# Keys and values of five of eight batches summed in pairs by accumulating DMAs instead of by GpSimd

## The chip, the cores and the metric

The kernel runs on one core of a Trainium2 chip. The metric is the device time of one execution in microseconds (us), told as the median of several runs; a profile is one further execution, and its span runs from the first to the last instruction. Engines are named as in the profile: PE is TensorE (matmuls; PEld its weight loads), DVE is VectorE, ACT is ScalarE, POOL is GpSimd, SP is SyncE. Each engine runs its own program strictly in order. DMAs issued by GpSimd or SyncE are carried out by 16 DMA engines that they share.

## What is computed

Inputs are q, k and v of shape 8 x 8 x 576 x 64 (batch, head, position, feature) in fp32, and four weight matrices. First comes attention with pooled keys and values, then a token and a channel MLP:

```python
k_p = k.reshape(B, H, Sp, pool, D).mean(axis=3)      # pool = 8, Sp = 72
v_p = v.reshape(B, H, Sp, pool, D).mean(axis=3)
scores = scale * np.matmul(q, k_p.transpose(0, 1, 3, 2))
...
attn = np.exp(scores)
attn = attn / (np.sum(attn, axis=-1, keepdims=True) + 1e-09)
attn_out = np.matmul(attn, v_p)
...
h = np.maximum(xt @ w_tok1, 0.0) @ w_tok2            # xt: x with tokens last
u = x + h.transpose(0, 2, 1)
h2 = np.maximum(u @ w_ch1, 0.0) @ w_ch2
out = u + h2
```

What matters here is the pooling: each pooled key (or value) is the mean of eight neighbouring rows of 64 numbers.

## The kernel before

**Units.** After a head for batch 0, the work goes in units 0 to 8. Unit n runs the channel MLP of batch n (`unit_steps`, matmuls of lines 438 and 461), 128x512 matmuls that fill TensorE. Unit 8 does the last tokens of all batches. Between its matmuls, a unit carries small steps of other batches: the attention and the token MLP of batch n+1, and the start of batch n+2. Tables (`FIRST` for unit 0, `SECOND` for unit 1, `THIRD` for unit 2, `LATER` from unit 3 on) say at which step of the unit which names are issued. A bare name means batch n+1, `<` batch n, `>` batch n+2; `lk3`, `lq3`, `lv3` mean the loads of k, q and v of batch n+3, `lv2` that of batch n+2. The order is written by hand (`manual_schedule`): every engine's program follows the order in which the steps are issued, and only the semaphores are put in by the framework.

**Loads.** `load_kv` fills a bf16 tile `kr` or `vr` of 72 partitions, with 8 heads x 8 rows x 64 numbers in each. Partition j holds the eight rows that pooled key j is made of. The load is one DMA, issued by GpSimd, that reads fp32 from HBM in pieces of 2,048 bytes and writes bf16 (line 86; batch 0 is cut in three). `load_q` loads q in the same way (line 103). Each of the three tiles has two buffers, so the load of batch b waits for the readers of batch b-2.

**Pooling.** `pool(eng, t, g)` pools four heads (g is 0 or 1) by `pool8`: add rows 0 to 3 to rows 4 to 7 (line 145, 72x1024 numbers out, fp32), add the halves of that (line 146, 72x512), and add the last two into `kp` or `vp` in bf16 (lines 149 and 151, 72x256). The names `K0 K1 V0 V1` do this on GpSimd, `k0 k1 v0 v1` on VectorE. VectorE does k1 and v1 of batch 1 and v1 of batch 2. From batch 3 on, all four are GpSimd's.

**Who needs it.** `kpT` (lines 194 and 196) transposes the pooled keys on TensorE and copies them to `kD` on VectorE; the scores `s0` to `s3` (line 254, exponent on ScalarE at line 260) read `kD` and the queries `qD` (line 243, `Q0` to `Q3`, VectorE). `av0` to `av4` (line 292) multiply the exponents by `vp`. All of these stand among the matmuls of the unit in TensorE's one program.

**GpSimd's program** around the change, from the tables: loads of batch 3 (FIRST step 20); K0, K1, V0 of batch 2 (FIRST steps 34 and 35); K0, K1 of batch 3 and the load of k of batch 4 (SECOND step 0); the loads of q and v of batch 4, then V0, V1 of batch 3 (SECOND step 1); then, in each of the units 2, 3 and 4, K0, K1, V0, V1 of batch n+2 and the loads of batch n+3 (step 0). GpSimd runs ahead of TensorE where nothing stops it. `spill` and `quads` (lines 372 and 379) move u through HBM in the later units, issued by SyncE: `mem` is written by one DMA and read by the next.

Of the kernel before, what the change touches and what calls it, by code (L numbers as in the profile page):

```python
# [8 lines left out]
FP32 = mybir.dt.float32  # L9
BF16 = mybir.dt.bfloat16  # L10
AF = mybir.ActivationFunctionType
ALU = mybir.AluOpType
# [8 lines left out]
def kernel(  # L21
# [14 lines left out]
    nc = tc.nc  # L36
    B, H, S, D = q.shape
    P = 128
    POOL = 8
# [40 lines left out]
    loaded = {}  # L80
# [4 lines left out]
    def kv(t, src, b, h0, h1, j0=0, j1=SP):  # L85
        nc.gpsimd.dma_start(out=t[j0:j1, h0:h1].rearrange("j h i d -> j h (i d)"),
                            in_=src[b, h0:h1].rearrange("h (j i) d -> j h (i d)", i=POOL)[j0:j1])

    def load_kv(b, src, key):
        t = loaded[b, key] = raw.tile([SP, H, POOL, D], BF16, name=key + "r")  # L90
        if b == 0:
            for h0, h1, j0, j1 in ((0, HP, 0, BP), (0, H, BP, SP), (HP, H, 0, BP)):
                kv(t, src, b, h0, h1, j0, j1)
        else:
            kv(t, src, b, 0, H)
# [12 lines left out]
    def load(key, b):  # L108
        if b < B:
            load_q(b) if key == "q" else load_kv(b, k if key == "k" else v, key)  # L110
# [31 lines left out]
    def pool8(eng, t, hs, dst, split):  # L142
        n = hs.stop - hs.start
        t4 = halves[eng is nc.vector]
        eng.tensor_tensor(out=t4[:, 0:n], in0=t[:, hs, 0:4], in1=t[:, hs, 4:8], op=ALU.add)  # L145
        eng.tensor_tensor(out=t4[:, 0:n, 0:2], in0=t4[:, 0:n, 0:2], in1=t4[:, 0:n, 2:4], op=ALU.add)  # L146
        if split:
            i0, i1 = (t4[:, 0:n, i].rearrange("j l (e d) -> j l e d", e=2) for i in range(2))
            eng.tensor_tensor(out=dst.rearrange("j e l d -> j l e d"), in0=i0, in1=i1, op=ALU.add)
        else:  # L150
            eng.tensor_tensor(out=dst, in0=t4[:, 0:n, 0], in1=t4[:, 0:n, 1], op=ALU.add)
# [3 lines left out]
    def batch_steps(b):  # L155

        par, first = b % 2, b == 0
        st = {}
# [26 lines left out]
        def pool(eng, t, g):  # L185
            def go():
                hs = slice(g * HP, (g + 1) * HP)
                pool8(eng, loaded[b, t], hs, st["kp"][:, g] if t == "k" else st["vp"][:, hs, 0:D], t == "k")
            return go

        def kpT():
# [383 lines left out]
```

## Time and profile before

| what | value | where from |
|---|---|---|
| median of three runs | 284.91 us (283.87 to 286.99) | the times |
| span of the profiled execution | 283.7 us | the page's first line |
| mean granted TensorE clock | 0.993 | the table of cores |
| DMA packets | 36,837, of which 18,672 on GpSimd's queue | the page's DMA part |
| HBM read, written | 38.21 MB, 11.80 MB | the page's DMA part |
| add of line 145 on GpSimd, keys, mean | 2,118 ns, 13 of them | the costliest groups |
| add of line 146 on GpSimd, mean | 1,332 ns, 25 of them | the costliest groups |
| add of line 149 on GpSimd, mean | 773 ns, 13 of them | groups by form |
| a load of k, q, v, issue to landing, median | 8.7, 11.9, 15.1 us | the DMA issues |

The page also shows the span in 40 slices of 7.1 us, each digit the busy share in tenths:

```profile
POOL 8684993999999929973993696000000000000000
PEclk9999979999999999999999999999999999999999
DMA  7999999951982397159748964514242346015014
```

GpSimd works in the first 25 slices and then has nothing left to do. The DMA engines are full for the first eight slices, while the weights and the first batches come in, and half full or less later. A line of the timeline begins with the start and the length in us; then come engine, line, operation, the tile that is written and those that are read, and in brackets how long the engine had been idle and what ended that. A line of the list of waits says who waited for what: us in total, times, longest.

### The profile page before, as it was taken

The page shows a single profiled execution, that of the slowest core. Times are in us where ns is not written, and L with a number is a line of the kernel's source. Part 1 is how long each engine was busy: PE and PEld are TensorE (multiplying, and loading weights), DVE is VectorE, ACT ScalarE, POOL GpSimd, SP SyncE. Part 2 cuts the span into 40 slices and gives each one's busy share as a digit, 9 for nine tenths or more (in the row PEclk, how much of TensorE's full clock was granted, in tenths as well). Part 3 has the DMA queues.
Part 4 walks back from the last instruction along what each step waited for, and adds up shares of the span by engine and source line. Part 5 has one row for each costly group of instructions (what it writes and reads, how often), then busy time and mean ns, then how long its engine had stood idle before and what let it go on. Part 6 is the DMA issues. An engine that isn't in the chain of part 4 may idle for free.

```text
span 283.7 us, 4529 instructions
## 1 busy us (share of the span) xinstructions
PE 273.8 (97%) x1816; PEld 130.9 (46%) x1816; DVE 149.4 (53%) x279; ACT 110.2 (39%) x193; POOL 138.1 (49%) x124
## 2 busy tenths in 40 slices
PE   8999879999999999999999999999999999999994
PEld 3855325443544445354435443544354444444443
DVE  5466975679657557474648464746474243011012
ACT  2543554009602643514561356135613511612600
POOL 8684993999999929973993696000000000000000
PEclk9999979999999999999999999999999999999999
DMA  7999999951982397159748964514242346015014
GB/s 158 193 202 208 204 202 186 217 121 40 124 138 64 74 127 126 37 78 200 162 75 137 231 165 52 112 39 122 45 96 55 102 64 136 16 37 112 2 39 109
DMA packets 36837, 32.68 MB, mean 115 GB/s; under 512 B 14288, under 2 KB 30288, under 8 KB 36816
## 3 DMA queue, kind: packets, MB, share of 16 engines
q0 software_dynamic: 18672, 17.64, 40.0%
q1 hardware_dynamic: 17984, 14.62, 21.8%
q8 instruction: 14, 0.23, 0.3%
q10 hardware_dynamic: 160, 0.13, 0.2%
q14 instruction: 7, 0.06, 0.1%
HBM read 38.21 MB, written 11.80 MB: 176 GB/s over the span
## 4 chain that ended last, share of the span: by engine, by line
PE 91%; DVE 5%; ACT 2%; issue 1%
PE p L461 31%; PE p L438 31%; PE p L353 6%; PE p L338 5%; PE p L254 4%; PE p L292 3%; PE pt L495 3%; ACT ex L260 2%; DVE qD L243 1%; PE pt L363 1%; DVE t L145 1%; PE p L450 1%; PE p L272 1%; PE p L321 1%; PE p L403 1%; PE p L225 1%
## 5 line engine op out<-in xcount | busy, mean ns | idle before, releaser
L461 PE MATMUL p<-w_ch,GT 128*128 128x512 bf16 x420 | 102.3, 380 | 0.0
L442 ACT ACTIVATE GT<-p 128x512 bf16<-128x512 f32 x108 | 64.3, 596 | 80.6 <-PE p L438 80.5
L438 PE MATMUL p<-uT,w_ch 128*128 128x512 bf16 x384 | 95.5, 382 | 0.0
L438 PEld LDWEIGHTS <-w_ch 128*128 128x128 bf16 x432 | 40.2, 98 | 47.9 <-issue 4.8
L461 PEld LDWEIGHTS <-GT 128*128 128x128 bf16 x420 | 37.6, 98 | 41.2 <-issue 3.5
L260 ACT ACTIVATE ex<-p 72x576 bf16<-72x576 f32 x56 | 33.1, 642 | 28.4 <-PE p L254 28.4
L145 POOL TENSOR_TENSOR t<-kr 72x1024 f32<-72x1024 bf16 x13 | 27.5, 2118 | 26.6 <-DMA kr<-in_k_dram 25.9
L466 DVE TENSOR_TENSOR o<-p,u 128x512 f32<-128x512 f32 x32 | 21.8, 682 | 32.3 <-PE p L461 32.2
L146 POOL TENSOR_TENSOR t<-t 72x512 f32<-72x512 f32 x25 | 33.3, 1332 | 2.0
L354 DVE TENSOR_TENSOR u<-p,x 128x512 bf16<-128x512 f32 x32 | 22.1, 691 | 13.7 <-PE p L353 13.7
L145 POOL TENSOR_TENSOR t<-vr 72x1024 f32<-72x1024 bf16 x12 | 25.5, 2123 | 0.8
L385 DVE STREAM_TRANSPOSE uT<-v 128x512 bf16<-128x512 bf16 x16 | 10.4, 685 | 22.0 <-DMA v<-mem 22.0
L310 DVE TENSOR_TENSOR x<-p,den 128x512 bf16<-128x512 f32 x30 | 20.7, 692 | 1.0
L243 DVE STREAM_TRANSPOSE qD<-qb 128x576 bf16<-128x576 bf16 x28 | 20.5, 789 | 0.0
L329 ACT ACTIVATE AT<-p 128x512 bf16<-128x512 f32 x8 | 4.8, 597 | 39.3 <-PE p L338 36.6
L292 PEld LDWEIGHTS <-ex 72*128 72x128 bf16 x320 | 15.4, 98 | 9.9 <-DVE x L310 0.8
L353 PE MATMUL p<-AT,w_tok 128*128 128x512 bf16 x64 | 19.0, 379 | 0.0
L292 PE MATMUL p<-vp,ex 72*128 72x65 bf16 x320 | 16.8, 194 | 0.5 <-DVE x L310 0.3
L254 PE MATMUL p<-qD,kD 32*72 32x288 bf16 x224 | 14.5, 306 | 2.0 <-DVE kD L196 1.8
L304 DVE RECIPROCAL den<-p 128x8 f32<-128x8 f32 (+1 forms) x39 | 8.0, 204 | 13.6 <-PE p L292 13.0
L338 PE MATMUL p<-x,w_tok 128*128 128x512 bf16 x56 | 14.4, 380 | 0.0
L331 DVE TENSOR_SCALAR AT<-p 128x512 bf16<-128x512 f32 x8 | 5.5, 692 | 13.7 <-PE p L338 12.9
(88 smaller groups left out, 207.3 us busy)
## 6 DMA issues: line engine op xcount, KB each, us to landing
out_dram<-o SPq DMA_DIRECT2D x70, 128.0 KB, 2.4
kr<-in_k_dram POOLq DMA_DIRECT2D x7, 576.0 KB, 8.7
qb<-in_q_dram POOLq DMA_DIRECT2D x7, 576.0 KB, 11.9
vr<-in_v_dram POOLq DMA_DIRECT2D x7, 576.0 KB, 15.1
w_ch<-in_moe_w_ch_dram POOLq DMA_DIRECT2D x6, 512.0 KB, 13.2
mem<-u SPq DMA_DIRECT2D x8, 256.0 KB, 2.1
v<-mem SPq DMA_DIRECT2D x8, 160.0 KB, 3.7
v<-mem SPq DMA_DIRECT2D x8, 128.0 KB, 3.4
```

The lines of the kernel that those rows point to most:

```text
L145: eng.tensor_tensor(out=t4[:, 0:n], in0=t[:, hs, 0:4], in1=t[:, hs, 4:8], op=ALU.add)
L146: eng.tensor_tensor(out=t4[:, 0:n, 0:2], in0=t4[:, 0:n, 0:2], in1=t4[:, 0:n, 2:4], op=ALU.add)
L243: nc.vector.transpose(out=late("qD")[:, g, db].rearrange("m (r j u) -> m u r j", u=2, r=BR), in_=st["qraw"][:, g].rearrange("m (u r d) -> ...
L254: nc.tensor.matmul(out=pss[l // 2][0:SP, l % 2, 0:SH], lhsT=st["kD"][quad, g, db, :], rhs=st["qD"][quad, g, db, half * SH:(half + 1) * SH] ...
L260: nc.scalar.activation(out=exv[:, h:h + 2], in_=pss[a][0:SP, :, 0:SH], func=AF.Exp, scale=scale)
L292: nc.tensor.matmul(out=halves[h // 4][:, (h % 4) * (D + 1):(h % 4 + 1) * (D + 1)], lhsT=st["ex"][:, h * S + n0:h * S + n0 + P], rhs=st["vp ...
L338: nc.tensor.matmul(out=ps, lhsT=w_tok1[:, c if c < 4 else 4 + par, m * P:(m + 1) * P], rhs=st["x"][:, c, :] if c < 4 else st["xt"], start= ...
L353: nc.tensor.matmul(out=ps, lhsT=w, rhs=a, start=(i == 0), stop=(i == len(mms) - 1))
L354: nc.vector.tensor_tensor(out=dst, in0=ps, in1=x, op=ALU.add)
L438: nc.tensor.matmul(out=ps, lhsT=w_ch1[:, kk, m * P:(m + 1) * P], rhs=uT[:, kk, :], start=(kk == 0), stop=(kk == 3))
L442: nc.scalar.activation(out=GT[:, m, :], in_=ps, func=AF.Relu)
L461: nc.tensor.matmul(out=ps, lhsT=GT[:, m, c * P:(c + 1) * P], rhs=w_ch2[:, m, :], start=(m == 0), stop=(m == NM - 1))
```

## The change

For batches 3 to 7, `load_kv` no longer loads bf16 rows. It sees the first half of the same tile as fp32, 8 heads x 128 numbers in a partition (`quarter_sums`). The eight rows of a pooled key are taken as four pairs; pair 0 is loaded by a plain fp32 DMA, and pairs 1, 2 and 3 are added to it by DMAs with `accum_op` add (`add_rows`). Each of these eight DMAs for k and v moves 72 x 8 pieces of 512 bytes. At the place of `lk3` only k's pair 0 is issued; at the place of `lv3` come v's pair 0 and then the six adds, k and v in turn. The load of q stays between them. In the tile then stand two sums of four rows, and `pool` does one add of 72x256 numbers, fp32 to bf16, on the engine that it had. Batches 0, 1 and 2 are as before.

```diff
+    summed = {}
+
+    def quarter_sums(b, key):
+        return loaded[b, key].rearrange("j h i d -> j (h i d)").bitcast(FP32)[:, 0:H * 2 * D].rearrange(
+            "j (h n) -> j h n", h=H)
+
+    def add_rows(b, key):
+        i = summed[b, key]
+        summed[b, key] = i + 1
+        src = (k if key == "k" else v)[b].rearrange("h (j i) d -> j h (i d)", i=POOL)
+        nc.gpsimd.dma_start(out=quarter_sums(b, key), in_=src[:, :, 2 * i * D:2 * (i + 1) * D],
+                            accum_op=ALU.add if i else ALU.bypass)
+
     def load_kv(b, src, key):
         t = loaded[b, key] = raw.tile([SP, H, POOL, D], BF16, name=key + "r")
+        if b >= 3:
+            summed[b, key] = 0
+            add_rows(b, key)
+            if key == "v":
+                for i in range(3):
+                    add_rows(b, "k")
+                    add_rows(b, "v")
+            return
...
         def pool(eng, t, g):
             def go():
                 hs = slice(g * HP, (g + 1) * HP)
-                pool8(eng, loaded[b, t], hs, st["kp"][:, g] if t == "k" else st["vp"][:, hs, 0:D], t == "k")
+                dst = st["kp"][:, g] if t == "k" else st["vp"][:, hs, 0:D]
+                if b < 3:
+                    pool8(eng, loaded[b, t], hs, dst, t == "k")
+                    return
+                pair = quarter_sums(b, t)[:, hs].rearrange("j l (i n) -> i j l n", i=2)
+                if t == "k":
+                    dst = dst.rearrange("j e l d -> j l e d")
+                    i0, i1 = (pair[i].rearrange("j l (e d) -> j l e d", e=2) for i in range(2))
+                else:
+                    i0, i1 = pair[0], pair[1]
+                eng.tensor_tensor(out=dst, in0=i0, in1=i1, op=ALU.add)
             return go
```

## The prediction

> **What bounds the kernel now.** I read the page's busy line first, then its chain of waits, then TensorE's waits after the start, and then GpSimd's timeline, because every line of the diff runs in GpSimd's program.
>
> ```profile
> PE 273.8 (97%) x1816; PEld 130.9 (46%) x1816; DVE 149.4 (53%) x279; ACT 110.2 (39%) x193; POOL 138.1 (49%) x124
> ...
> PE 91%; DVE 5%; ACT 2%; issue 1%
> ```
>
> TensorE is busy for 97% of the span and holds 91% of the chain; GpSimd (POOL) is busy for half. TensorE's waits from 45 us to the end, all that are over 150 ns:
>
> ```profile
> PE pt L194 <- DVE uT_tails L364: 0.5, 1, 0.5
> PE pt L194 <- DVE ex L166: 0.5, 1, 0.5
> PE pt L194 <- DVE uT L364: 0.2, 1, 0.2
> ```
>
> So after 45 us TensorE waits for 1.2 us in all. That caps what any relief of GpSimd or VectorE can bring at 1.2 us, or 0.4%. The waits before 45 us belong to batches 0 and 1, which the diff leaves alone. The question is only whether the change makes something late. GpSimd's timeline from 38 to 60 us:
>
> ```profile
> 38.58 1.59 POOL L151 TENSOR_TENSOR vp<-t 72x256 bf16<-72x256 f32 x1
> 40.12 0.86 POOL L86 DMA_DIRECT2D kr<-in_k_dram  x1
> 40.97 0.73 POOL L103 DMA_DIRECT2D qb<-in_q_dram  x1
> 41.68 0.84 POOL L86 DMA_DIRECT2D vr<-in_v_dram  x1
> 47.32 2.12 POOL L145 TENSOR_TENSOR t<-kr 72x1024 f32<-72x1024 bf16 x1 [4.79 <-DMA kr<-in_k_dram]
> 49.51 1.26 POOL L146 TENSOR_TENSOR t<-t 72x512 f32<-72x512 f32 x1
> 50.85 0.72 POOL L149 TENSOR_TENSOR kp<-t 72x256 bf16<-72x256 f32 x1
> 51.65 2.12 POOL L145 TENSOR_TENSOR t<-kr 72x1024 f32<-72x1024 bf16 x1
> ```
>
> The three issues are the loads of batch 3 (`lk3 lq3 lv3`, FIRST step 20). Behind them in the same program stand K0 and K1 of batch 2 (FIRST step 34). Each takes 4.1 us in three adds; K0 starts at 47.32, when its keys land, and K1 ends at 55.9. Who needs them, in the timeline around 63 us:
>
> ```profile
> 63.12 0.29 PE L194 MATMUL pt<-ident,kp 72*128 72x72 bf16 x4 [0.46 <-DVE ex L166]
> ...
> 63.45 0.31 DVE L196 COPY kD<-pt 128x288 bf16<-128x288 bf16 x1 [0.32 <-PE pt L194]
> ```
>
> This is kpT of batch 2, first in SECOND. TensorE runs its program in order, so all its work waits for K1 of batch 2. The slack there is 63.1 - 55.9 = 7.2 us. The same subtraction for the later batches, 3 to 7, with the ends of K1 at 70.1, 89.8, 114.7, 140.5 and 166.5 and their kpT at 88.2, 114.2, 139.6, 168.6 and 196.7, gives slacks of 18 to 30 us. Batch 2 is the tight place.
>
> **What is removed.** For batches 3 to 7, twenty pools lose their first two adds: 20 x (2.12 + 1.26) = 68 us of GpSimd work. It lies beside matmuls, and nobody on TensorE waits for it: worth 0 to 1.2 us by the waits above; I take 0. The one add left reads 72x256 fp32 pairs like line 149's row, 0.72 us, or 0.8 with the gap after it.
>
> **What is added.** Each batch has eight DMAs of 72 x 8 rows of 512 B in place of two, so GpSimd issues nine per batch with q's, five times. The issue of 576 rows costs 0.85 us now; six more are 5.1 us a batch. More important are the waits. An add must not start before the earlier transfer into the same bytes has landed. The trace shows an issuing queue doing just this where a DMA needs another's data (`v<-mem` after `mem<-u`):
>
> ```profile
> SPq L379 <- DMA mem<-u: 8.9, 4, 3.8
> ```
>
> I take it that GpSimd likewise stops, in its own program, until the earlier k or v part has landed, and everything behind it stops too. The Trainium skill's "DMA: Bandwidth & Descriptors", section "Rules for kernel authors", speaks against the change here: an accumulating DMA beside another access to the same bytes must wait for the earlier one's semaphore; no row of this trace shows an accumulating DMA.
>
> **Price of one add.** No such transfer is in the trace, so I bound it. Parts: k of batch 4, issued at 70.09 into idle queues, landed after 7.8 us, and batch 5's after 7.5. In the trace's packet records its 1024 B packets (2048 B read) take 98 ns each, and 15 engines work on them at once, 40 rows each: 3.9 us. The rest, about 3.7 us, is issue, start and receipt. Packets of 512 B that read 1024 B (line 121's) take 60 ns. On that straight line a plain row of 512 B takes 41 ns, so a first part is 40 x 41 = 1.6 us; an add reads 512 B and the old 512 B, so I take the 60 ns row: 2.4 us, and 3.7 + 2.4 = 6.1 us from issue to landing. Upper end: two reads one after the other, 120 ns, 4.8 us, landing 8.5 us. Lower end: the 256 KB of `mem<-u` land in 2.1 us, though from the SyncE queue and towards HBM. I take 6.1, since GpSimd-issued loads of the same rows are nearest.
>
> **Batch 3, step by step.** The queue is backed up at 40 us: v of batch 2, issued at 34.14, lands 17.0 us later, at 51.1 (the load's time to landing). Behind it: k's first part 52.7, q 56.0 (3.3 us, as batch 3's q lands after its k now), v's first part 57.6. Then, with each DMA issued when its predecessor has landed and the rings serving one after the other: k's first add 52.7 to 60.0, v's 57.6 to 63.7; k's second to 66.1, v's to 69.8; k's third issued at 66.1, v's at 69.8, done at 70.7. Only now does K0 of batch 2 start. K0 and K1 take what they take now, 55.9 - 47.3 = 8.6 us, and end at 79.3. kpT of batch 2 moves from 63.1 to 79.3: **16.2 us of TensorE idle**. Then comes the clock: after today's 2.9 us of TensorE waiting (34.6 to 37.4) the granted clock shows
>
> ```profile
> 37.00:40.50 3.50, 3.05 (x20) 0.83 (x20) 3.46 (x4) 1.67 (x3) 3.34 (x4) 0.51 1.25 205
> ```
>
> which is a stretch table whose third number from the end is the clock: half speed for 3.4 us. Matmuls after the new stall lose half of that, 1.7 us (0 if VectorE covers it). Sum 17.9 us.
>
> By the fit in the skill's same page, section "Anatomy of one DMA", 2.0 us plus bytes over 436 GB/s, an add of 295 KB would land in an estimated 2.7 us. The trace's 7.5 us for a load, of which 3.7 fixed, speaks for more; by the fit K0 would start near 64.9 and the sum would be 12 us, 297 in time.
>
> **What is late next.** V0 of batch 2 ends at 83.7, with av0 8.5 us behind kpT: hidden. K0 and K1 of batch 3, 1.6 us, end at 85.3. Then the load of batch 4 holds GpSimd: first parts at 90.6 and 95.5, v's adds 101.6 and 107.7, last issue done at 108.6. V0 and V1 of batch 3 stand behind it (SECOND step 1) and end at 110.1; their reader av0 is at 95.8 now, so at 113.7 then: hidden by 3.6 us only. From there a batch costs GpSimd 30.1 us (waits, issues, four adds) against about 28.5 us per batch on TensorE (kpT at 139.6, 168.6, 196.7). Batches 5, 6 and 7 are pooled at 141.8, 171.9 and 202.0 for kpT due at 157.5, 186.5 and 214.6: hidden by 16, 15 and 13 us. So TensorE pays once, in unit 1, and the shift stays to the end.
>
> **Sum.** Span 283.7 + 17.9 = 301.6. The runs' median, 284.91, lies 1.2 above the profiled span (which is near the lowest run, 283.87), so the time is **303 us**.
>
> **Rivals.**
> *GpSimd's chain binds later units too.* If one add needs over 7.9 us, the 3.6 us above are gone (two rounds stand in that sum, 1.8 us each). At 7.3 us a batch costs 33.7 and batch 7 alone is late, by 2 us: 308. At the upper end (4.8 us of transfer, so 9.6 us a round for k and v) a batch costs 40.6: the first stall is 23.2, av0 of batch 3 is 3.5 late, batches 6 and 7 about 11 each, with the clock's losses 55 in all: 340. For it: k and v share the rings, and SyncE's output stores, which the change leaves in place, take up to 0.3 of the same engines. Chance 0.2.
> *A short stall.* Adds land in 2.1 to 3 us, like `mem<-u`: K0 starts near 64, stall 9 to 11, 294 to 297. Against it stand the 7.5 us loads. Chance 0.08.
> *Not slower: the adds wait for nothing.* If the issues go out back to back, six more cost 5.1 us, GpSimd is free at 47.6 in place of 42.5, and K0 of batch 2, whose keys land at 47.2 anyway, starts 0.3 later, inside 7.2 us of slack. Time 284 to 285, at best 1.2 us lower. It decides if three rounds take less than about 13 us from 42.5 on, so that K0 starts before 54.5. The waits on `mem` speak against it; shorter work on GpSimd (49% busy, never the bound) speaks for it only if the waits fall away. Chance 0.08, of which 0.03 for over 1% faster, for which I see no row.
>
> **Numbers.** The forecast (one stall, 299 to 307) has 0.64. The range, 294 to 330, leaves out the rival with no waits and some of the short stall (about 0.1), and the upper part of the chain that binds (about 0.1). A measurement of this kernel tells about 1% from no change. Faster 0.03, same 0.05, slower 0.92.
>
> **What would show it.** In the changed profile: GpSimd idle between 42 and 70 us in waits for `kr` and `vr`; K0 of batch 2 starting near 70; kpT (line 194's successor) waiting for GpSimd by about 16 us, with a slice of low granted clock after it; no other TensorE wait over 2 us; GpSimd's work ending near 205. I am wrong if K0 of batch 2 still starts before 54, if an add lands outside 2 to 8.5 us, or if TensorE waits again at kpT of batches 6 and 7.

## The result, and the profile after

The changed kernel takes 312.06 us (median of four runs, 310.70 to 316.18); the kernel before, on the same chip, 285.95. The ratio is 1.090, with a 95% interval of 1.083 to 1.098: slower by 26 us. The medians here and below are over all runs of a kernel, while the ratios leave out, on both sides, runs that lie over 1.5% above their kernel's fastest. The profiled execution of the changed kernel spans 310.4 us, 26.7 more than before. All line numbers below are those of the changed kernel; line 225 is the old 194 (kpT), 323 the old 292 (av), 99 issues the new DMAs.

From the page, with cuts marked: busy time and count, the granted clock and the busy share of the DMA engines in 40 slices of 7.8 us, and the chain by engine.

```profile
PE 280.8 (90%) x1816; PEld 132.1 (43%) x1816; DVE 148.2 (48%) x279; ACT 110.4 (36%) x193; POOL 112.3 (36%) x114
...
PEclk9999869985599999999999999969999999999999
DMA  8999999994078989796999899991333263304114
...
PE 60%; DMA 16%; POOL 10%; issue 7%; DVE 4%; SPq 1%; ACT 1%; DVEq 0%; POOLq 0%
```

GpSimd has 26 us less to do, and TensorE, which held 91% of the chain, holds 60%: transfers and GpSimd stand in it now. The clock dips at slices 10 and 11 and again at slice 27; the dip at slices 5 and 6 lies in the head, where the kernel before has one at slice 6. TensorE's list of waits has grown at two places:

```profile
PE pt L225 <- POOL kp L170: 15.8, 3, 10.7
PE p L323 <- DVE x L341: 5.8, 3, 3.8
```

The first is kpT of batch 2 (14.7 of the 15.8; the rest is batch 1's, as before). The second is av in units 3 and 4: 1.6 and 3.8 us (the third wait, 0.3 us, is in the head). Subtracting the start of each batch's kpT before from that after (for batch 2 after, the start of its second half) shows where the time is lost:

| kpT of batch | before | after | later by | new in this stretch |
|---|---|---|---|---|
| 2 | 63.1 | 78.7 | 15.6 | the stall of unit 1 |
| 3 | 88.2 | 106.4 | 18.1 | 2.5, half clock after the stall |
| 4 | 114.2 | 132.3 | 18.1 | |
| 5 | 139.6 | 157.8 | 18.1 | |
| 6 | 168.6 | 188.6 | 20.0 | 1.8, wait at av in unit 3 |
| 7 | 196.7 | 223.5 | 26.8 | 6.8, wait at av in unit 4 and half clock |
| end of span | 283.7 | 310.4 | 26.7 | |

TensorE waits 14.7 us at kpT of batch 2; it had come to it 1.0 us later than before, out of the head.

**The first loss.** The timeline of GpSimd's program while it loads batch 3, up to the second half of kpT of batch 2:

```profile
41.90 0.85 POOL L99 DMA_DIRECT2D vr<-in_v_dram  x1
52.91 1.41 POOL L99 DMA_DIRECT2D kr<-in_k_dram  x1 [10.17 <-DMA kr<-in_k_dram]
55.85 1.39 POOL L99 DMA_DIRECT2D vr<-in_v_dram  x1 [1.53 <-DMA vr<-in_v_dram]
59.68 1.38 POOL L99 DMA_DIRECT2D kr<-in_k_dram  x1 [2.44 <-DMA kr<-in_k_dram]
62.47 1.39 POOL L99 DMA_DIRECT2D vr<-in_v_dram  x1 [1.41 <-DMA vr<-in_v_dram]
66.13 1.39 POOL L99 DMA_DIRECT2D kr<-in_k_dram  x1 [2.28 <-DMA kr<-in_k_dram]
68.72 1.37 POOL L99 DMA_DIRECT2D vr<-in_v_dram  x1 [1.20 <-DMA vr<-in_v_dram]
69.56 2.67 POOL L166 TENSOR_TENSOR t<-kr 72x1024 f32<-72x1024 bf16 x1
...
74.42 0.30 PE L225 MATMUL pt<-ident,kp 72*128 72x72 bf16 x2 [10.71 <-POOL kp L170]
...
78.74 0.30 PE L225 MATMUL pt<-ident,kp 72*128 72x72 bf16 x2 [4.02 <-POOL kp L170]
```

Each add waits for its own tile's transfer before (the brackets), and K0 of batch 2, the line at 69.56, stands behind all six. It started at 47.32 before.

**The second loss.** The chain of waits in unit 4, start and length:

```profile
185.62 5.08 DMA mem<-u
...
192.32 7.44 DMA v<-mem
...
199.88 0.16 DVE uT L416
...
204.28 0.70 DVE x L341
...
205.03 0.62 PE p L323 x8
```

u of batch 5 goes to HBM and back, which takes 14.1 us here, from the issue of the last `mem<-u` to the landing of the last `v<-mem`; it took 8.0 before (165.65 to 173.63). The DMA engines are fuller in this stretch: their busy share is 1.18 from 185.6 to 199.8 us (above 1 where packets overlap in time), and it was 0.67 before, from 165.6 to 173.7; for the round trip in unit 3 it is 1.02 where it was 0.64. VectorE waits for it in order (line 416). Its other work behind that, the division at line 341 among it, comes late, and av waits for the PSUM tiles that line 341 frees.

### The profile page after: what moved, and what is told of

It reads as the page before. It is cut to its first block, busy times and chain, and to the rows that moved or that the text cites. A ratio compares the mean times of both kernels' runs of the same rounds, so it can differ in the third digit from the quotient of the medians.

```text
span 310.4 us, 4512 instructions
## 1 busy us (share of the span) xinstructions
PE 280.8 (90%) x1816; PEld 132.1 (43%) x1816; DVE 148.2 (48%) x279; ACT 110.4 (36%) x193; POOL 112.3 (36%) x114
## 4 chain that ended last, share of the span: by engine, by line
PE 60%; DMA 16%; POOL 10%; issue 7%; DVE 4%; SPq 1%; ACT 1%; DVEq 0%; POOLq 0%
PE p L469 24%; PE p L492 21%; DMA v<-mem 5%; DMA vr<-in_v_dram 4%; DMA kr<-in_k_dram 4%; PE p L384 4%; PE p L369 4%; POOL t L166 3%; DMA mem<-u 2%; PE p L323 2%; PE p L285 2%; POOL t L167 2%; SPq L410 1%; DVE uT L416 1%; POOL vr L99 1%
## 5 line engine op out<-in xcount | busy, mean ns | idle before, releaser
L492 PE MATMUL p<-w_ch,GT 128*128 128x512 bf16 x420 | 104.6, 386 | 0.0
L469 PE MATMUL p<-uT,w_ch 128*128 128x512 bf16 x384 | 99.2, 393 | 0.0
L469 PEld LDWEIGHTS <-w_ch 128*128 128x128 bf16 x432 | 40.9, 100 | 50.3 <-issue 8.9
L99 POOL DMA_DIRECT2D kr<-in_k_dram x20 | 25.2, 1260 | 42.2 <-DMA kr<-in_k_dram 42.2
L99 POOL DMA_DIRECT2D vr<-in_v_dram x20 | 25.1, 1257 | 31.7 <-DMA vr<-in_v_dram 31.7
L323 PEld LDWEIGHTS <-ex 72*128 72x128 bf16 x320 | 15.8, 101 | 16.6 <-DVE x L341 7.9
L225 PE MATMUL pt<-ident,kp 72*128 72x72 bf16 x28 | 2.5, 203 | 16.5 <-POOL kp L170 15.8
L335 DVE RECIPROCAL den<-p 128x8 f32<-128x8 f32 (+1 forms) x39 | 7.9, 203 | 18.1 <-PE p L323 17.7
L362 DVE TENSOR_SCALAR AT<-p 128x512 bf16<-128x512 f32 x8 | 5.5, 691 | 13.4 <-PE p L369 12.6
```

Of the source, the lines that this page charges most:

```text
L99: nc.gpsimd.dma_start(out=quarter_sums(b, key), in_=src[:, :, 2 * i * D:2 * (i + 1) * D], accum_op=ALU.add if i else ALU.bypass)
L323: nc.tensor.matmul(out=halves[h // 4][:, (h % 4) * (D + 1):(h % 4 + 1) * (D + 1)], lhsT=st["ex"][:, h * S + n0:h * S + n0 + P], rhs=st["vp ...
L469: nc.tensor.matmul(out=ps, lhsT=w_ch1[:, kk, m * P:(m + 1) * P], rhs=uT[:, kk, :], start=(kk == 0), stop=(kk == 3))
L492: nc.tensor.matmul(out=ps, lhsT=GT[:, m, c * P:(c + 1) * P], rhs=w_ch2[:, m, :], start=(m == 0), stop=(m == NM - 1))
```

## The experiments

Each was run beside the kernel before on the same chip; the edits shown are against the changed kernel, with cuts marked. "Over before" is the difference of medians.

| run | median us | ratio to before, 95% interval |
|---|---|---|
| changed kernel | 312.06 | 1.090 (1.083 to 1.098) |
| from4 | 299.39 | 1.047 (1.039 to 1.055) |
| last_plain | 306.70 | 1.074 (1.067 to 1.082) |
| apart_plain | 295.79 | 1.034 (1.028 to 1.041) |
| busy | 313.97 | 1.100 (1.092 to 1.107) |
| two | 304.30 | 1.055 (1.046 to 1.065) |
| same_plain | 303.46 | 1.063 (1.055 to 1.071) |
| order | 300.28 | 1.052 (1.045 to 1.060) |
| first_parts67 | 308.02 | 1.083 (1.075 to 1.091) |
| no_spill34 | 306.97 | 1.075 (1.065 to 1.085) |
| from4_v | 299.99 | 1.040 (1.028 to 1.052) |
| busy2 | 314.50 | 1.097 (1.087 to 1.107) |
| both_out | 288.70 | 1.011 (1.004 to 1.018) |

**from4: batch 3 as before.**

```diff
-        if b >= 3:
+        if b >= 4:
...
-                if b < 3:
+                if b < 4:
```

> Adds for batches 4 to 7 only; batch 3 is loaded and pooled as before. Theory A (TensorE's stall in unit 1 comes from batch 3's waiting adds, which stand ahead of K0 and K1 of batch 2 in GpSimd's program): K0 of batch 2 starts near 47 again, the 14.3 us stall and its 3 us of half clock go, and what stays is the later loss of about 8 us: 8 to 10 over before, 294 to 296. Rival B (the adds' transfers slow the whole kernel through the DMA engines, wherever they stand): four fifths of the 26 us stay, near 307. Rival C (the later loss follows from the first stall): 286 to 288.

Measured: 299.39, 12.7 over before. K0 of batch 2 starts near 46 and the stall at its kpT is gone, so theory A holds for this stall, and B and C fall. But the time is 3 us above A's upper end. TensorE's waits in this run:

```profile
PE p L323 <- POOL vp L172: 5.6, 2, 4.0
PE p L323 <- DVE x L341: 4.8, 3, 3.8
```

The first line is new: av of batch 3 now waits for V0 and V1 of batch 3, which stand behind the load of batch 4 (SECOND step 1) and still take three adds each. That is the same mechanism, one batch on, with half clock for 6.8 us (95.8 to 102.7).

**last_plain: batches 6 and 7 as before.**

```diff
-        if b >= 3:
+        if 3 <= b < 6:
...
-                if b < 3:
+                if not 3 <= b < 6:
```

> Adds for batches 3 to 5 only; 6 and 7 are loaded and pooled as before. Theory D (the two waits of TensorE at av in units 3 and 4, 1.6 and 3.8 us, and the half clock after the second, 3 us, come from the round trip of u through HBM, v<-mem, which is carried by the same DMA engines while the adds of batches 6 and 7 run): those waits go, v<-mem lands within 9 us of the last mem<-u again, the stall of unit 1 stays: 17 to 19 over before, 303 to 305. Rival (they come from GpSimd's late pools or from the first stall): 311 to 313.

Measured: 306.70, 20.0 over before, 1.7 us above the range. kpT of batch 2 comes 16.3 us later than before, much as in the changed kernel. The waits at av shrink to 1.0 and 1.3 us, with no half clock after them, but they don't go, and the round trips take 11.9 and 11.6 us, not 9: plain loads of 1.2 MB of fp32 each also stood in the rings (the queues of the DMA engines) while u went out (`mem<-u` issued at 152.7 landed at 160.1).

**apart_plain: no part waits for another.**

```diff
...
-        nc.gpsimd.dma_start(out=quarter_sums(b, key), in_=src[:, :, 2 * i * D:2 * (i + 1) * D],
-                            accum_op=ALU.add if i else ALU.bypass)
+        dst = quarter_sums(b, key, i) if i < 2 else apart[key, i].rearrange("j (h n) -> j h n", h=H)
+        nc.gpsimd.dma_start(out=dst, in_=src[:, :, 2 * i * D:2 * (i + 1) * D],
+                            accum_op=ALU.bypass)
```

> Batches 3 to 7: all four parts of k and v are plain DMAs into four places of their own, so that no part waits for another; the bytes read and the number of DMAs stay. The sums over the four parts are left out: the one add pools the first part alone. Theory A (the waits between the adds are the cost): GpSimd is held only by the issues and the eight-deep queue, K0 of batch 2 starts at 51 to 55 and its K1 ends by 63: no stall in unit 1, 286 to 291. Rival B (number of DMAs and bytes): 305 to 312.

Measured: 295.79, 9.1 over before. The step in question came out as theory A said: the last issue of batch 3 starts at 53.3 and TensorE waits 1.4 us at kpT of batch 2 in place of 14.7. The total missed A's range by 4.8 us, and one wait of 6.8 us at av in unit 3, with half clock after it, is more than that: the eight plain DMAs now stand in the rings together, and one `v<-mem`, issued at 141.5, landed at 155.6. So the second loss needs no accumulating DMA.

**busy and busy2: TensorE kept busy through the stall.**

```diff
-    SECOND = {0: "kpT Q0 Q1 >K0 >K1 lk3", 1: "Q2 Q3 v1 lq3 lv3 >V0 >V1", 4: "s0", 6: "s1", 9: "s2", 12: "s3", 14: "av0", 16: "av1",
+    SECOND = {0: "w60 kpT Q0 Q1 >K0 >K1 lk3", 1: "Q2 Q3 v1 lq3 lv3 >V0 >V1", 4: "s0", 6: "s1", 9: "s2", 12: "s3", 14: "av0", 16: "av1",
...
+                if s[0] == "w":
+                    head("d" + s[1:])
+                    continue
```

> As changed, with 60 matmuls of 128x512 without use (12.9 us at full clock) ahead of kpT at the start of unit 1, inside the stall of 14.3 us. If the half clock after the stall costs 3 us (6 us of matmuls at half rate after 78.7), the clock stays full and the time falls by 2.5 to 3.5 us against the changed kernel, to 308 to 310. If VectorE covers that stretch, as my lower bound had it, the time stays at 311 to 313.

Measured: 313.97, no gain, and inconclusive: the added matmuls ended before the second part of the stall, and the clock fell in it and stayed at half from 77.5 to 84.3. busy2 therefore also puts 21 matmuls between the two halves of kpT of batch 2.

```diff
...
             for i in range(4):
+                if b == 2 and i == 2:
+                    idle = ps_one.tile([P, 512], FP32, name="p1")
+                    for _ in range(21):
+                        nc.tensor.matmul(out=idle, lhsT=warm[:, 0:P], rhs=warm, start=True, stop=True)
```

> The changed kernel with matmuls without use both ahead of kpT of batch 2 (60) and between its first and second pair of transposes (21, 4.5 us), so that TensorE is busy through both parts of the stall. The clock should stay full after 78 (it fell in the run with the first 60 alone, in the second part of the stall). If the half clock costs about 3 us: 308.5 to 310.5; if VectorE covers that stretch: 311.5 to 313.

Measured: 314.50, outside both ranges, so the total decides nothing. The stretch does. In busy2 the window from 78 to 107 us shows (clock third from the end):

```profile
78.00:107.00 29.00, 28.76 (x204) 13.68 (x203) 17.38 (x31) 11.69 (x21) 18.49 (x15) 1.00 0.51 83
```

From the last transpose of kpT of batch 2 to that of batch 3 it takes 25.1 us (81.9 to 107.0), exactly as before the change (63.2 to 88.3), against 27.7 in the changed kernel (78.8 to 106.5). The half clock costs 2.6 us, and VectorE does not cover it. In this execution the stall itself ended 3 us later, and the waits at av took 2.7 and 4.1 us in place of 1.6 and 3.8: what was gained in one place was lost in others.

**two: one round of adds.**

```diff
...
-        nc.gpsimd.dma_start(out=quarter_sums(b, key), in_=src[:, :, 2 * i * D:2 * (i + 1) * D],
+        nc.gpsimd.dma_start(out=quarter_sums(b, key), in_=src[:, :, 4 * i * D:4 * (i + 1) * D],
...
-                for i in range(3):
+                for i in range(1):
...
-                pair = quarter_sums(b, t)[:, hs].rearrange("j l (i n) -> i j l n", i=2)
+                t4 = halves[eng is nc.vector]
+                four = quarter_sums(b, t)[:, hs].rearrange("j l (i n) -> j l i n", i=4)
+                eng.tensor_tensor(out=t4[:, :, 0:2], in0=four[:, :, 0:2], in1=four[:, :, 2:4], op=ALU.add)
+                pair = [t4[:, :, i] for i in range(2)]
```

> Batches 3 to 7 in two parts of four rows (pieces of 1,024 B): one plain load and one add for k and for v, and two adds of GpSimd left in place of one. Theory A (the number of rounds that GpSimd waits through sets the stall): the first parts land by 57, one add each, K0 of batch 2 starts near 59, its K1 ends near 67.5: kpT of batch 2 about 4.5 later than before in place of 15.6; with up to 3 us of half clock and 1 to 4 us at the spills 6 to 11 over before, 292 to 297. Rival (an accumulating transfer is slow in itself, by its bytes): the same bytes are added, the stall shrinks by less than half, 302 or more.

Measured: 304.30, with runs from 298.89 to 307.72 (the profiled one is the fastest); a miss. kpT of batch 2 is 8.6 later than before, not 4.5. The first part of v (576 KB) landed at 61.4, where that of 288 KB had landed at 55.6, and the adds of 576 KB took 10.7 and 8.1 us to land. So rounds are not all: part of an add's price grows with its bytes (the first of the two also ran beside the end of v's first part). Yet with one round in place of three kpT of batch 2 came 7.0 us earlier than in the changed kernel (15.6 to 8.6 late). TensorE's wait there shrank by less, from 14.7 to 10.2, because in this execution it came to it 2.5 us earlier.

**same_plain: the waits without the adding.**

```diff
-                            accum_op=ALU.add if i else ALU.bypass)
+                            accum_op=ALU.bypass)
```

> All eight DMAs of a batch plain, each part into the same place as the one before it, so the waits stay and nothing is added; the sums over the parts are left out (the last part alone is pooled). If the wait for a landing is most of the price and the adding itself little: each part lands in about 4.5 us like k's first part in place of 6.0 to 6.4, and its issue takes 0.85 in place of 1.39: K0 of batch 2 starts near 66, kpT of batch 2 is 11 to 12 later than before, in all 15 to 20 over before, 301 to 306. If the adding is most of it: parts land in under 3 us, the stall is below 6, under 296.

Measured: 303.46, within the range. Issues take 0.81 us, k's parts land in 4.9 to 5.3 us, and kpT of batch 2 is 12.3 later than before. Of 15.6 us, the adding, with its longer issues and landings, accounts for 3.3, the waits for landings for most of the rest (apart_plain, without them, leaves 1.4 us of waiting).

**order: the pools first.**

```diff
-             16: "s0", 18: "s1", 20: "s2 lk3 lq3 lv3", 22: "s3", 24: "av0", 26: "av1", 28: "av2", 30: "av3", 32: "av4",
-             34: "at0 >K0 >K1", 35: "at1 >V0", 37: "u0", 38: "u1", 39: "u2", 40: "t0", 41: "u3", 42: "t1 u4", 44: "t2", 45: "t3",
+             16: "s0", 18: "s1", 20: "s2", 22: "s3", 24: "av0", 26: "av1", 28: "av2", 30: "av3", 32: "av4",
+             34: "at0 >K0 >K1", 35: "at1 >V0 lk3 lq3 lv3", 37: "u0", 38: "u1", 39: "u2", 40: "t0", 41: "u3", 42: "t1 u4", 44: "t2", 45: "t3",
...
-    SECOND = {0: "kpT Q0 Q1 >K0 >K1 lk3", 1: "Q2 Q3 v1 lq3 lv3 >V0 >V1", 4: "s0", 6: "s1", 9: "s2", 12: "s3", 14: "av0", 16: "av1",
+    SECOND = {0: "kpT Q0 Q1 >K0 >K1 lk3", 1: "Q2 Q3 v1 >V0 >V1 lq3 lv3", 4: "s0", 6: "s1", 9: "s2", 12: "s3", 14: "av0", 16: "av1",
```

> The change, with the loads of batch 3 moved behind K0, K1 and V0 of batch 2 (FIRST step 35), and V0, V1 of batch 3 ahead of the loads of q and v of batch 4 (SECOND step 1). Theory A: K0 of batch 2 starts near 47, no wait at its kpT. But batch 3's load then begins at 60, and GpSimd's chain (29 to 34 us a batch) has lost the slack that the first stall gave it: TensorE waits a few us each at kpT of batches 4 to 7, in all 9 to 16 over before, 295 to 302. Rival (order does not matter, the work of the adds does): 311 to 313. If GpSimd's chain stays hidden as the prediction had it (slack of 13 us or more): the spills alone, 291 to 295.

Measured: 300.28, 15.0 over before, within A's range. K0 of batch 2 is on time, and the waits move on:

```profile
PE pt L225 <- POOL kp L219: 9.2, 4, 4.3
PE p L323 <- DVE x L341: 2.1, 2, 1.6
```

The first line is kpT of batches 5 and 7, up to 4.3 us each: GpSimd takes 31 to 33 us from the load of one batch to the next (83.9, 115.5, 146.7, 179.3), TensorE 28 to 29 before the change. Batch 4's load starts at 83.9, close to the changed kernel's 85.8, while TensorE is some 18 us earlier here (kpT of batch 3 at 87.8, not 106.4). The prediction's hidden 13 to 16 us were there only because the first stall held TensorE back.

**first_parts67: little traffic for batches 6 and 7.**

```diff
-            if key == "v":
+            if key == "v" and b < 6:
```

> The change, but for batches 6 and 7 only the first part of k and v is loaded, the adds are left out (so their pooled values are of two rows). Theory D (traffic of batches 6 and 7 delays the round trip of u): with a quarter of that traffic v<-mem lands within 9 us of the last mem<-u, as before, no wait at av in units 3 and 4, the stall of unit 1 stays: 17.5 to 20 over before, 304 to 306; below the run with plain loads for batches 6 and 7 (306.7), which still waited 1.0 and 1.3 us there. Rival (those waits have another cause on VectorE): both waits stay, 309 to 312.

Measured: 308.02, between the two ranges. The wait in unit 4 is gone (`v<-mem` 193.3 to 198.8 with no load beside it), but the one in unit 3 grew to 4.2 us: without batch 6's adds, GpSimd issued batch 7's load at 158.6, right beside `v<-mem` (158.4 to 170.2). The trace's packet records show the two side by side: from 162 to 166 us, 498 packets of 256 B of `v<-mem` next to 220 of 2,304 B and 38 of 4,096 B, 125 small packets a us; before the change, alone in the rings, some 430 a us (2,560 from 168 to 174). I had reduced the traffic, and moved the rest to the worst moment. The load beside it here is plain, as in apart_plain and last_plain: the round trip is slowed by loads without adds too.

**no_spill34: u not through HBM in units 3 and 4.**

```diff
+    MIDDLE = {i: " ".join(x for x in s.split() if x[0] not in "MT") for i, s in LATER.items()}
+    for i, x in ((6, "t0"), (7, "t1"), (9, "t2"), (13, "t3"), (16, "t4")):
+        MIDDLE[i] = (MIDDLE.get(i, "") + " " + x).strip()
...
-            unit(n, LATER)
+            unit(n, MIDDLE if n in (3, 4) else LATER)
```

> The change, but u of batches 4 and 5 is transposed by TensorE in units 3 and 4 (steps t0 to t4, as units 1 and 2 do) and no longer goes through HBM there. Theory D (the waits at av in those units come from v<-mem, held up in the DMA rings by whatever load runs beside it): no wait at av in units 3 and 4, no half clock after 200; kpT of batch 2 as late as in the changed kernel (15 to 16). The transposes cost TensorE about 0.22 us for each of 9 blocks, 2 us in all. 18 + 2 = 20 over before, 304 to 307, 5 to 7 below the changed kernel. Rival (the waits come from GpSimd or from VectorE's own work): the waits stay, 312 to 315.

Measured: 306.97, at the top of the range. The stall of unit 1 stays (kpT of batch 2 is 17.5 us later than before, batch 3's load having been issued 1.9 us later than in the changed kernel), the waits at av in units 3 and 4 are gone (the 0.3 is in the head), and the clock is full from 85 us to the tail:

```profile
PE pt L225 <- POOL kp L170: 17.6, 3, 11.9
...
PE p L323 <- DVE x L341: 0.3, 1, 0.3
```

The batches' adds and GpSimd's waits are as in the changed kernel; the round trip is taken away, for TensorE's transposes. From kpT of batch 2 to the end, 4.3 us are lost against the kernel before in place of 11.1: 2.0 in the half clock after the stall and 2.3 between kpT of batches 4 and 6, where the transposes stand. This settles theory D.

**from4_v: V0 and V1 of batch 3 ahead of the load of batch 4.**

```diff
-        if b >= 3:
+        if b >= 4:
...
-                if b < 3:
+                if b < 4:
...
-    SECOND = {0: "kpT Q0 Q1 >K0 >K1 lk3", 1: "Q2 Q3 v1 lq3 lv3 >V0 >V1", 4: "s0", 6: "s1", 9: "s2", 12: "s3", 14: "av0", 16: "av1",
+    SECOND = {0: "kpT Q0 Q1 >K0 >K1 lk3", 1: "Q2 Q3 v1 >V0 >V1 lq3 lv3", 4: "s0", 6: "s1", 9: "s2", 12: "s3", 14: "av0", 16: "av1",
```

> Adds for batches 4 to 7 only, as in the run before (299.4), and V0, V1 of batch 3 moved ahead of the loads of q and v of batch 4 (SECOND step 1). Theory A, extended: the waits of 1.5 and 4.0 us at av of batch 3 and the half clock there (3 us) came from these pools standing behind the adds of batch 4; they go, the later waits (0.7 and 3.8 us and 1.7 of clock) stay: 5 to 8 over before, 291 to 294. Rival (they have another cause): 298 to 301.

Measured: 299.99, a miss, in the rival's range, though the rival's reason does not hold: the waits at av of batch 3 did go. Those of units 3 and 4 grew to 4.4 and 8.2 us in the profiled execution (301.19, the slowest of the four; the fastest took 295.93), with half clock after both: loads and round trips now coincide (one `v<-mem` took 14.7 us to land, the longest seen). The price of the second loss depends on when they meet.

**both_out: both causes removed, adds kept for batches 4 to 7.** Its edits are those of from4_v and no_spill34 together.

> The last two together: adds for batches 4 to 7 only, V0 and V1 of batch 3 ahead of the loads of batch 4, and u of batches 4 and 5 transposed by TensorE in units 3 and 4. If the two causes (pools of an earlier batch behind waiting adds in GpSimd's program; v<-mem held up by loads in the DMA rings) are all of the loss, TensorE waits nowhere over 1 us after 60 us and the clock stays full: 2 us of transposes and nothing else, 1 to 4 over before, 287 to 290, though 36 DMAs of adds and their waits are still made. If something else in the adds costs time, 293 or more. It does not beat the kernel before by either theory.

Measured: 288.70, 3.9 over before; within the range. From TensorE's list of waits:

```profile
PE p L285 <- DVE kD L227: 2.0, 1, 2.0
PE pt L225 <- POOL kp L170: 1.3, 1, 1.3
...
PE p L323 <- DVE x L341: 0.6, 1, 0.6
```

All three lie in the head, before 40 us (at 38.5, 35.3 and, 0.55 of the last, 18.6); after 60 us no wait is over 0.6 us, and the clock stays full from 44 us to the tail. The accumulating DMAs of four batches (24; the 36 of the expectation counts all that GpSimd issues for them), and GpSimd's waits for them, are still there and cost nothing that shows: of the 4.2 us by which the profiled span is longer than before, 1.9 arise in the head, before kpT of batch 2, 2.3 between kpT of batches 4 and 6, where the transposes stand, and none anywhere else. No version here beats the kernel before.

## Why the prediction was right or wrong

**Direction and first loss: right, by its own steps.** GpSimd stops for each landing; K0 of batch 2 starts at 69.6 (predicted 70.7); kpT of batch 2 is 15.6 us late (16.2). from4, order and apart_plain each took away one condition of this step (batch 3's adds, their place, their waits), and the stall went with each, but for 1.4 us in apart_plain.

**The price of an add: right in sum.** The medians from issue to landing, against 6.1:

```profile
kr<-in_k_dram POOLq DMA_DIRECT2D x20, 288.0 KB, 6.0
vr<-in_v_dram POOLq DMA_DIRECT2D x20, 288.0 KB, 6.4
```

(Each median is over one first part and three adds a batch; over the 30 adds alone it is 6.1.) Its packets of 512 B take 65 ns in the median where 60 was taken. One sign of being wrong did come up: the adds issued at 156.3 and 190.4, beside the round trips of u, landed after 9.5 and 8.5 us, the first of them outside the 2 to 8.5 us that the prediction allowed. Two parts were off in opposite directions: an add's issue takes 1.39 us, not 0.85, and v's first part landed at 55.6, not 57.6; the records show a plain part mostly in packets of 4,096 B, where rows of 512 B had been taken. The estimate of 2.7 us by the fit of the Trainium skill's "DMA: Bandwidth & Descriptors" (section "Anatomy of one DMA") is below all of the adds (5.4 us is the shortest), and the measurement decides.

**The half clock: mis-sized.** It was put at 1.7 us (3.4 us at half rate); it lasted 6 us after the stall and cost 2.6 (busy2). The stretch table of the changed kernel, for the time after each of the two losses:

```profile
78.70:84.80 6.10, 6.06 (x22) 1.78 (x22) 5.66 (x8) 2.86 (x5) 5.88 (x4) 0.50 0.00 1
...
204.20:211.00 6.80, 5.97 (x35) 2.96 (x36) 4.73 (x11) 0.00 (x0) 2.81 (x4) 0.50 0.80 155
```

**What failed** is the step "So TensorE pays once, in unit 1, and the shift stays to the end." GpSimd's chain was as hidden as it said: the pools of k of batches 5, 6 and 7 ended at 139.9, 173.3 and 206.3 (141.8, 171.9, 202.0 predicted) for kpT at 157.8, 188.6 and 223.5. But the prediction looked only for late pools, and took SyncE's transfers for a load on the adds, never the adds for a load on SyncE's transfers. The round trip of u had its own reader on VectorE, and TensorE's av behind that. It was in the profile before; the first line is from there, the second from the changed kernel:

```profile
DVE uT L385 <- DMA v<-mem: 22.0, 4, 7.9
DVE uT L416 <- DMA v<-mem: 31.7, 4, 10.6
```

Nor were the DMA engines "half full or less" after the start, as the text ahead of the prediction has it: their line there shows shares of 0.7 to 0.9 in eight of the slices from 11 to 23.

How much the round trip could grow can be read from all the traces together. In the ten that have a wait at av in unit 3, the wait is the length of the round trip less 10.9 us (12.6 us give 1.6 in the changed kernel, 17.7 give 6.8 in apart_plain); in the nine that have one in unit 4, it is that length less 10.3 us (14.1 give 3.8, and 18.5 give 8.2 in from4_v), all to within 0.1 us. Before, the two round trips took 9.1 and 8.0 us, so they had 1.9 and 2.4 us to spare. (In order a trip of 11.4 us in unit 3 cost nothing; TensorE had just waited 4.0 us at kpT.)

The second loss is 8.6 of the 26.7 us: 1.8 in unit 3, and 6.8 in unit 4 with its half clock; the prediction's sign "no other TensorE wait over 2 us" failed there, with 3.8. no_spill34 and both_out show it by taking the round trip away. So the forecast of 303 was 9 too low, and its own stretch, 299 to 307, was missed. The measured time lies within the wider range by luck: what set the range's upper part was another rival, a chain of GpSimd's that binds.

The Trainium skill's "DMA: Bandwidth & Descriptors", section "Queues, rings and completion order", says that each DMA engine takes turns between its queues packet by packet. The packet counts under first_parts67 agree with it as far as they go: in those 4 us both queues move on, 498 small packets of one beside 258 larger ones of the other. The records do not name the engine of a packet, so turns one by one are not shown.

**The rivals.** *The adds wait for nothing* fell with the brackets in GpSimd's timeline. *A short stall* fell with 6.0 us to landing. *GpSimd's chain binds later units* did not occur in the changed kernel, but did in order, where TensorE comes early enough to wait for it.

## What to carry to other kernels

A DMA that adds to bytes which an earlier one still writes costs its issuing engine a wait for that landing (same_plain: so does one that overwrites them), so ask what stands behind those waits in that engine's program, and who needs it next; here it was the pools K0 and K1 of another batch, and kpT of that batch came 15.6 us late. When a load is cut into several transfers, list every other transfer that runs beside it and what its reader has to spare, not only the readers of the load. And a stall removed moves the others: order gave back part of its gain at the next place, and from4_v is not clearly faster than from4 (1.040 and 1.047, with intervals that overlap).

## What the runs showed of the hardware

- An accumulating DMA of 576 pieces of 512 B is issued in 1.37 to 1.41 us on GpSimd in the changed kernel, a plain one in 0.85 to 0.88 there and in 0.81 mostly in same_plain, and the records show 8-byte packets beside the adds, about 190 an add, that plain transfers don't have.
- A plain fp32 part of the same pieces, whose target is contiguous in each partition, shows up mostly as packets of 4,096 B (172 ns in the median in the changed kernel); the adds there show up as packets of 512 B (65 ns).
- The granted clock after the stall of 14.7 us stayed at half for 6 us of nearly unbroken matmuls, and in busy it fell within a wait of 4.1 us. After a wait of 3.8 us in unit 4 it stayed at half for 6.8 us in the changed kernel and for 3.4 us in from4 and busy; the wait of 1.6 us in unit 3 left it full. Its stretches in these traces are multiples of 3.4 us (3.41, 6.83, 17.07 us), so what a stall costs here depends on where it falls in them.
